# Splitting x two steps behind its load, and issuing ScalarE's transfers from GpSimd, in a fused linear-attention and feed-forward kernel

## Chip, cores, metric

One core of a Trainium2 chip. The metric is the device time of one execution in microseconds, as the median of several. The profile is a trace of one execution; its span is mostly some 1.8 us shorter than that execution's device time.

## The reference, cut to what matters

```python
def _attn_ref(q, k, v, alpha):            # (4, 8, 768, 48) each
    for t in range(S):
        state = alpha[:, :, t, :, None] * state + np.einsum('bhd,bhe->bhde', k[:, :, t], v[:, :, t])
        y[:, :, t] = np.einsum('bhd,bhde->bhe', q[:, :, t], state)

def _moe_ref(x, w1, w2, w3, w_out):       # x (3072, 384), w1 and w2 (384, 1024)
    a = x @ w1
    b = x @ w2
    h = a * b @ w3
    return h @ w_out
```

The attention's output, reshaped to 3072 tokens of 384, is the x of the second part. All is float32; the weights arrive as 64-bit floats.

## The kernel before

Part one walks over 24 chunks of 128 tokens. Step n makes the scores of chunk n, the attention of chunk n-1, the logarithms of n+4, the decays of n+3, and so on. Three chunks make a group of x (384 tokens, in DRAM tile `xd`). In part one a finished group is loaded back every four steps, beginning at step 4, split into three float32r parts, and fed to "gates" (tiles of `x @ w1` times `x @ w2`), which fill TensorE's spare time in later steps. A gate runs in two halves; `run(k)` advances k halves. `convert` advances the work that turns a weight tile from 64-bit words to float32 parts on DVE and ACT.

```python
    def decays(n):
        ...                                                          # a matmul on the logarithms la
        nc.scalar.activation(e[:, 0], lc, AF.Exp, scale=-1.0)        # L259
        nc.scalar.activation(e[:, 1], lc, AF.Exp)                    # L260
        if n in ends:
            nc.scalar.dma_start(out=ends[n][0:1], in_=e[0:1, 0])
    ...
    def split_x(g, i):
        x = st.pop(("xT", g))
        t = tr[i].tile([C, 3, KM, TG], FP32R, tag="x3", name="x3")   # one buffer in part one
        st["x3", g] = t
        nc.scalar.activation(t[:, 0], x, AF.Copy, scale=1.0 - 2.0 ** -13)             # L376
        nc.vector.tensor_sub(t[:, 1], x, t[:, 0].bitcast(FP32))                       # L377
        nc.vector.scalar_tensor_tensor(t[:, 2], t[:, 0].bitcast(FP32), 1.0 + 1.0 / P, x,
                                       op0=ALU.mult, op1=ALU.subtract)                # L378
    ...
    begin = {4 + 4 * g: (g, range(FH if g < 4 else KF)) for g in range(5)}
    for n in range(N + 1):
        ...
        if n < N:
            scores(n)                       # L330 on TensorE: its start marks step n below
        transposed(n + 1)                   # L290 on TensorE, L292 copies qkT on ACT
        if n - 1 in begin:
            g, tiles = begin[n - 1]
            split_x(g, 0)
            fill.extend(gate(g, f) for f in tiles)
        ...
        if n:
            attend(n - 1)                   # stores y to xd
        outer(n)
        run(n - 1 not in begin)
        decayed(n + 2)                      # L268 on DVE
        logs(n + 4)                         # L238 on ACT
        if n in begin:
            load_x(begin[n][0], nc.scalar)  # L370
        run(1)
        decays(n + 3)
        ...
        run(n - 1 in begin)
```

The framework that builds the kernel decides in which order the instructions of one engine stand in that engine's queue.

Of the kernel before, what the change touches and what calls it, by code (L numbers as in the profile page):

```python
# [48 lines left out]
def kernel(  # L49
# [12 lines left out]
    nc = tc.nc  # L62
    B, H, S, D = q.shape
    C = 128
# [5 lines left out]
    DP = 64  # L70
# [30 lines left out]
    def bank():  # L101
        return ps.tile([C, 512], FP32, tag="bank", name="bank")
# [6 lines left out]
    ends = {n: dram.tile([3, DM], FP32, name=f"ends{n}") for n in range(2, N, 2) if n % NCH}  # L109
# [11 lines left out]
    def load_a(n):  # L121
        if n < N:
            st["a", n] = inp.tile([C, H, D], FP32, tag="ac", name="ac")
            nc.sync.dma_start(out=st["a", n], in_=rows(alpha, n))

    def load_kq(n):
        if n >= N:
            return
        st["kq", n] = inp.tile([C, 2, H, D], FP32, tag="kq", name="kq")
        nc.sync.dma_start(out=st["kq", n][:, 0], in_=rows(k, n))  # L130
        nc.sync.dma_start(out=st["kq", n][:, 1], in_=rows(q, n))

    def load_v(n):
        if n < N:
            st["v", n] = vs[n % len(vs)]
            nc.sync.dma_start(out=st["v", n][:, :, 0:D], in_=rows(v, n))
# [22 lines left out]
    decs = [p1.tile([C, 3, NP], FP32, name=f"dec{i}") for i in range(2)]  # L159
# [54 lines left out]
    def convert(steps, ahead=3):  # L214

        for _ in range(steps):
            while weights and len(begun) < ahead:
                begun.append(weights.popleft())
                next(begun[-1])
            if not begun:  # L220
                return
            x = begun.popleft()
            try:
                next(x)
                begun.appendleft(x)
            except StopIteration:
                pass
# [5 lines left out]
    def logs(n):  # L233
        if n >= N:
            return
        a = st.pop(("a", n)).rearrange("p h d -> p (h d)")
        la = st["la", n] = work.tile([C, DM], FP32, tag="la", name="la")
        nc.scalar.activation(la, a, AF.Ln)  # L238
        if n >= LATE:

            t = st["la", n] = work.tile([C, 2, DM], FP32R, tag="la2", name="la2", bufs=1)
            nc.scalar.copy(t[:, 0], la)
            nc.vector.tensor_sub(t[:, 1], la, t[:, 0].bitcast(FP32))
        if n in ends:
            nc.scalar.dma_start(out=ends[n][2:3], in_=a[0:1])

    def decays(n):
        if n >= N:
            return
        lc = bank()[:, 0:DM]  # L250
        la = st.pop(("la", n))
        if n < LATE:
            nc.tensor.matmul(lc, utri if n % 2 else after, la, start=True, stop=True)
        else:
            for i in range(2):
                nc.tensor.matmul(lc, sums[:, n % 2], la[:, i], start=(i == 0), stop=(i == 1))  # L256

        e = st["e", n] = work.tile([C, 2, DM], FP32, tag="e", name="e", bufs=3)
        nc.scalar.activation(e[:, 0], lc, AF.Exp, scale=-1.0)  # L259
        nc.scalar.activation(e[:, 1], lc, AF.Exp)  # L260
        if n in ends:
            nc.scalar.dma_start(out=ends[n][0:1], in_=e[0:1, 0])
        if n + 1 in ends:
            nc.scalar.dma_start(out=ends[n + 1][1:2], in_=e[C - 1:C, 1])

    def decayed(n):
        if n < N:
# [3 lines left out]
    def load_ends(n):  # L271
        if n not in ends:
            return
        with nc.allow_non_contiguous_dma(reason="single values to partitions"):
            for i in range(2):
                nc.scalar.dma_start(out=decs[n // 2 % 2][ds(DP * i, D)].rearrange("d m j -> d (m j)"),
                                    in_=ends[n].rearrange("m (j i d) -> i d (m j)", i=2, d=D)[i])

    def transposed(n):
# [58 lines left out]
    def attend_state(n):  # L338
        qkT = st.pop(("qkT", n))



        y = [bank()[:, 0:HP * C].rearrange("p (j c) -> p j c", c=C) for _ in range(2)]
        st["y", n] = y, [(half * HP + j, i, y[i][ds(DP * half, DP), j, :])
                         for j in range(HP) for i in range(2) for half in range(2)]
        if n % NCH:
            for j, i, to in st["y", n][1]:
                r = ds(DP * i, D)
                nc.tensor.matmul(to, Ts[n % 2][r, j, :], qkT[r, 1, j, :],  # L349
                                 start=(j % HP == 0), stop=False, skip_group_check=True)  # L350

    def attend(n):
        (y, heads), ms, vc = st.pop(("y", n)), st.pop(("ms", n)), st.pop(("v", n))
        for j, i, to in heads:
            nc.tensor.matmul(to, vc[:, 2 * j + i, :], ms[:, i, j, :], start=(n % NCH == 0 and j % HP == 0),  # L355
                             stop=(j % HP == HP - 1), skip_group_check=True)
        x = work.tile([C, HP, 2, C], FP32, tag="x", name="x")
        for i in range(2):
            nc.scalar.copy(x[:, :, i], y[i])
        x = x.rearrange("p j i t -> p (j i) t")  # L360

        g, c = divmod(n, G)
        to = xd[g].rearrange("(b h d) t -> b d h t", b=2, d=D)
        for half in range(2):
            nc.scalar.dma_start(out=to[half, :, :, ds(c * C, C)], in_=x[ds(DP * half, D)])


    def load_x(g, queue=nc.sync):
        st["xT", g] = xp.tile([C, KM, TG], FP32, tag="xT", name="xT")
        queue.dma_start(out=st["xT", g], in_=xd[g].rearrange("(k p) t -> p k t", p=C))  # L370
# [10 lines left out]
    def exact(to, w, x, scale):  # L381

        p1, p2 = (bank()[:, 0:to.shape[1]] for _ in range(2))
        n = len(w[0])
        for part in range(2):
            for i in range(n):
                nc.tensor.matmul(p1, w[part][i], x[part][i], start=(part == i == 0), stop=(part == 1 and i == n - 1))  # L387
        t = gw.tile(list(to.shape), FP32, tag="t", name="t")
        nc.scalar.activation(t, p1, AF.Copy, scale=(1.0 + 1.0 / P) * scale)  # L389
        for i in range(n):  # L390
            nc.tensor.matmul(p2, w[2][i], x[2][i], start=(i == 0), stop=(i == n - 1))  # L391
        nc.vector.scalar_tensor_tensor(to, p2, -scale, t, op0=ALU.mult, op1=ALU.add)  # L392

    def gate(g, f):
        r = []
        x = [[st["x3", g][:, part, kk, :] for kk in range(KM)] for part in range(3)]
        for i, scale in enumerate((1.0, P * P)):
            r.append(gw.tile([C, TG], FP32, tag="r", name="r"))
            exact(r[-1], [[w12[:, part, i, kk, ds(f * C, C)] for kk in range(KM)] for part in range(3)], x, scale)
            if len(r) == 1:  # L400
                yield
        ab = abp.tile([C, TG], FP32, tag="ab", name="ab")
        nc.vector.tensor_mul(ab, *r)  # L403
        store_ab()
        st["ab"] = g, f, ab

    def store_ab():
        if "ab" in st:
            g, f, ab = st.pop("ab")
            nc.sync.dma_start(out=abd[g][:, f, :], in_=ab)  # L410
# [57 lines left out]
    def run(pieces):  # L468

        for _ in range(pieces):  # L470
            if not fill:
                return
            try:
                next(fill[0])
            except StopIteration:
                fill.popleft()
# [18 lines left out]
    load_kq(3)  # L495
    load_a(4)

    begin = {4 + 4 * g: (g, range(FH if g < 4 else KF)) for g in range(5)}

    for n in range(N + 1):  # L500
        load_v(n + AHEAD - 1)
        load_a(n + 5)
        load_kq(n + AHEAD)
        if n:
            attend_state(n - 1)
        if n < N:
            scores(n)
        transposed(n + 1)
        if n - 1 in begin:
            g, tiles = begin[n - 1]  # L510
            split_x(g, 0)
            fill.extend(gate(g, f) for f in tiles)
        if n == 0:
            logs(2)
            decays(2)
            logs(3)
        early = n < 7
        convert(1, 2 if n == 0 else 3)
        advance(n)
        if n:  # L520
            attend(n - 1)
        outer(n)
        run(n - 1 not in begin)
        if early:
            convert(1)
        decayed(n + 2)
        logs(n + 4)
        if n in begin:
            load_x(begin[n][0], nc.scalar)
        convert(early and n > 2)  # L530
        run(1)
        decays(n + 3)
        load_ends(n + 2)
        convert(early or n % 3 == 0)
        run(n - 1 in begin)
    part1.close()


# [78 lines left out]
```

## Time and profile before

| | before |
|---|---|
| device time, median of the first 3 runs | 507.94 us (507.48 to 508.53) |
| span of the profile | 506.9 us |
| PE busy | 466.6 us (92%), so 40.3 us idle |
| DVE, ACT, POOL busy | 371.3, 248.1, 13.8 us |
| mean granted TensorE clock | 0.973 |

The profile's lines are in the prediction. Read them for PE alone: from 215 us on PE is busy without gaps, but for one wait of 1.0 us at 403 us (L387 for `ab`, L454). So a change to part one can do little more than bring the start of that stretch forward.

### The profile page before, as it was taken

To read this page: it belongs to the slowest core of one execution; us is meant where nothing else is said; L and a number is where in the kernel's file an instruction comes from. 1 tells how busy PE (TensorE), PEld (TensorE's weight loads), DVE (VectorE), ACT (ScalarE), POOL (GpSimd) and SP (SyncE) were. 2 spreads that over 40 slices of the span, in tenths; PEclk is the share of its full clock that TensorE was granted. 3 is DMA by queue.
4 is the path that set the end of the run, shared out by engine and by line. 5 is a ranking of instruction groups with operands and counts; after the bars stand their busy time and mean duration, and the time that the engine had idled before them with its cause. 6 is when DMAs were issued, how large, how long until landed. Compare 5 with 4: busy or idle time off the path is not lost.

```text
span 506.9 us, 9883 instructions
## 1 busy us (share of the span) xinstructions
PE 466.6 (92%) x3760; PEld 424.8 (84%) x3760; DVE 371.3 (73%) x620; ACT 248.1 (49%) x479; POOL 13.8 (3%) x43
## 2 busy tenths in 40 slices
PE   3777499499799999999999999999999999999997
PEld 1556388398799899899999998898888799999996
DVE  2777789699966767599999976967533497777771
ACT  2665566468557555355555544544323343333330
POOL 2000000010100010000000000000000000000000
PEclk9998599889899999999999999999999999999999
DMA  9999999998879833265565432432001686555511
GB/s 173 182 217 196 256 216 225 194 246 209 166 167 215 194 81 106 79 186 174 177 200 186 160 117 88 142 103 72 33 31 48 171 231 192 174 180 179 174 56 47
DMA packets 168735, 79.10 MB, mean 156 GB/s; under 512 B 112856, under 2 KB 162544, under 8 KB 168688
## 3 DMA queue, kind: packets, MB, share of 16 engines
q1 hardware_dynamic: 147184, 70.73, 54.9%
q10 hardware_dynamic: 21504, 7.75, 6.7%
q8 instruction: 29, 0.48, 0.4%
q14 instruction: 18, 0.15, 0.1%
HBM read 56.40 MB, written 22.06 MB: 155 GB/s over the span
## 4 chain that ended last, share of the span: by engine, by line
PE 71%; DVE 1%; issue 0%; ACT 0%; DVEq 0%
PE bank L387 36%; PE bank L391 18%; PE bank L436 8%; PE bank L355 2%; PE bank L330 2%; PE bank L430 1%; PE bank L349 1%; PE bank L290 1%; PE bank L302 1%; PE bank L256 1%; DVE x L378 1%; DVE x L377 0%; ACT t L389 0%; ACT ab L454 0%; DVE r L392 0%
## 5 line engine op out<-in xcount | busy, mean ns | idle before, releaser
L387 PE MATMUL bank<-x,w 128*128 128x384 f32 x768 | 163.9, 348 | 15.0 <-DVE x L377 8.5
L387 PEld LDWEIGHTS bank<-x,w 128*128 128x128 f32 x768 | 136.5, 192 | 21.1 <-DVE x L377 9.7
L389 ACT ACTIVATE t<-bank 128x384 f32<-128x384 f32 x152 | 73.4, 490 | 119.2 <-PE bank L387 96.7
L392 DVE SCALAR_TENSOR_TENSOR r<-bank,t 128x384 f32<-128x384 f32 x128 | 68.4, 550 | 45.7 <-ACT t L389 37.1
L391 PE MATMUL bank<-x,w 128*128 128x384 f32 x384 | 89.2, 340 | 1.5 <-DVE x L378 1.4
L391 PEld LDWEIGHTS bank<-x,w 128*128 128x128 f32 x384 | 69.2, 191 | 3.1 <-PE bank L387 1.4
L387 PE MATMUL bank<-w3o,ab 128*128 128x384 f32 x384 | 70.6, 335 | 1.0 <-ACT ab L454 1.0
L387 PEld LDWEIGHTS bank<-w3o,ab 128*128 128x128 f32 x384 | 66.8, 188 | 1.4 <-ACT ab L454 1.3
L436 PE MATMUL bank<-wo,w3T 128*128 128x384 f32 x128 | 42.6, 486 | 0.0
L391 PE MATMUL bank<-w3o,ab 128*128 128x384 f32 x192 | 37.1, 334 | 0.0
L436 PEld LDWEIGHTS bank<-wo,w3T 128*128 128x128 f32 x128 | 24.2, 189 | 14.9
L189 ACT ACTIVATE rest<-raw 128x512 f32<-128x512 uint32 (+1 forms) x36 | 23.4, 649 | 26.6 <-DMA raw<-in_moe_w_dram 18.3
L455 DVE TENSOR_TENSOR ab<-abl,ab 128x1024 fp32r<-128x1024 f32 x24 | 29.4, 1223 | 9.1 <-ACT ab L454 9.1
L403 DVE TENSOR_TENSOR ab<-r 128x384 f32<-128x384 f32 x64 | 35.3, 552 | 0.9
L454 ACT ACTIVATE ab<-abl 128x1024 fp32r<-128x1024 f32 x24 | 25.5, 1062 | 20.1 <-PE bank L391 18.8
L330 PEld LDWEIGHTS bank<-qkT 48*128 48x128 f32 x384 | 25.5, 198 | 10.8 <-ACT qkT L292 5.1
L330 PE MATMUL bank<-qkT 48*128 48x128 f32 x384 | 30.7, 298 | 4.2 <-ACT qkT L292 3.7
L333 DVE TENSOR_TENSOR ms<-bank,keep 128x512 int32<-128x512 int32 x48 | 31.2, 682 | 4.2 <-PE bank L330 4.2
L391 PEld LDWEIGHTS bank<-w3o,ab 128*128 128x128 f32 x192 | 33.6, 188 | 0.0
L292 ACT COPY qkT<-bank 128x512 f32<-128x512 f32 x48 | 25.8, 586 | 10.3 <-PE bank L290 8.8
L194 ACT ACTIVATE power<-power,rebias 128x512 uint32<-128x512 uint32 (+1 forms) x36 | 25.0, 696 | 10.3 <-DVE power L193 10.3
L392 DVE SCALAR_TENSOR_TENSOR o<-bank,t 128x384 f32<-128x384 f32 x24 | 13.4, 556 | 22.1 <-issue 13.7
(65 smaller groups left out, 509.7 us busy)
## 6 DMA issues: line engine op xcount, KB each, us to landing
abd<-ab SPq DMA_DIRECT2D x64, 192.0 KB
abl<-abd SPq DMA_DIRECT2D x24, 512.0 KB
raw<-in_moe_w_dram SPq DMA_DIRECT2D x16, 512.0 KB
raw<-in_moe_w_dram SPq DMA_DIRECT2D x24, 256.0 KB
ac<-in_alpha_dram SPq DMA_DIRECT2D x24, 192.0 KB
kq<-in_k_dram SPq DMA_DIRECT2D x24, 192.0 KB
kq<-in_q_dram SPq DMA_DIRECT2D x24, 192.0 KB
v<-in_v_dram SPq DMA_DIRECT2D x24, 192.0 KB
```

Of the source, the lines that this page charges most:

```text
L194: nc.scalar.activation(power, power, AF.Relu, scale=2.0 ** 23, bias=rebias)
L292: nc.scalar.copy(qkT[:, :, :, ds(DP * half, DP)], tp[half])
L330: nc.tensor.matmul(sc[i][:, j, :], qkT[r, 0, j, :], qkT[r, 1, j, :], start=True, stop=True)
L333: nc.vector.tensor_tensor(ms[:, i].bitcast(I32), sc[i].bitcast(I32), keep_bc, op=ALU.bitwise_and)
L387: nc.tensor.matmul(p1, w[part][i], x[part][i], start=(part == i == 0), stop=(part == 1 and i == n - 1))
L389: nc.scalar.activation(t, p1, AF.Copy, scale=(1.0 + 1.0 / P) * scale)
L391: nc.tensor.matmul(p2, w[2][i], x[2][i], start=(i == 0), stop=(i == n - 1))
L392: nc.vector.scalar_tensor_tensor(to, p2, -scale, t, op0=ALU.mult, op1=ALU.add)
L403: nc.vector.tensor_mul(ab, *r)
L436: nc.tensor.matmul(po, w3T[:, j, :], wo[:, j, :], start=(j == 0), stop=(j == KF - 1))
L454: nc.scalar.activation(t[:, 0], ab, AF.Copy, scale=1.0 - 2.0 ** -13)
L455: nc.vector.tensor_sub(t[:, 1], ab, t[:, 0].bitcast(FP32))
```

## The change

Its intent: give the split of x a whole step of slack after the load, so that PE never stands before a gate whose x isn't split, keep gates out of the step that splits, and take the issuing of transfers out of ScalarE's queue. All 93 transfers of ScalarE move.

```diff
-            nc.scalar.dma_start(out=ends[n][2:3], in_=a[0:1])
+            nc.gpsimd.dma_start(out=ends[n][2:3], in_=a[0:1])
 ... the same at the stores of e, the loads of dec, the stores to xd and load_x
-        if n - 1 in begin:
-            g, tiles = begin[n - 1]
+        if n - 2 in begin:
+            g, tiles = begin[n - 2]
             split_x(g, 0)
             fill.extend(gate(g, f) for f in tiles)
+        pieces = (0, 3, 3, 2)[(n - 6) % 4] if n > 5 else 0
 ...
-        run(n - 1 not in begin)
+        run(pieces > 0)
 ...
-        run(1)
+        run(pieces > 1)
 ...
-        run(n - 1 in begin)
+        run(pieces > 2)
```

## The prediction

> **What bounds the kernel now.** I read the page first (part 4, then part 2), then PE's waits, PE's instructions in order of time, and last the busy table of chosen stretches. The chain that ended last is nearly all TensorE, so an idle or slow microsecond of PE is a microsecond of the kernel:
>
> ```profile
> PE 71%; DVE 1%; issue 0%; ACT 0%; DVEq 0%
> PE   3777499499799999999999999999999999999997
> DMA  9999999998879833265565432432001686555511
> ```
>
> From slice 17 on (215 us) PE is full; four dips lie before that, under a DMA row that is full up to slice 10. The waits of PE from 40 to 215 us name the dips:
>
> ```profile
> PE bank L387 <- DVE x L377: 8.5, 3, 4.8
> PE bank L387 <- ACT x L376: 6.5, 2, 4.8
> PE bank L391 <- DVE x L378: 1.4, 2, 0.8
> ```
>
> That is 16.4 us of PE waiting for the split of x (one ACT copy, two DVE operations), out of some 20 us idle in that stretch. In order of time, PE's rows at the second split (the first row is the last attention work of the step):
>
> ```profile
> 92.29 0.62 PE L302 MATMUL bank<-v,qk 128*64 128x48 f32 x16
> 94.65 0.79 PE L387 MATMUL bank<-x,w 128*128 128x384 f32 x3 [1.74 <-ACT x L376]
> 100.28 1.33 PE L387 MATMUL bank<-x,w 128*128 128x384 f32 x3 [4.84 <-DVE x L377]
> ```
>
> The gates stand in PE's queue in the same step as the split, and PE takes its queue in order, so the next chunk's attention waits too. Taking the start of each score group (L330) as the start of step n, the split steps 5, 9, 13, 17, 21 last 18.6, 17.4, 12.0, 8.0 and 7.0 us, against 7.3 of an ordinary step with one gate. **The excess is 11.3 + 10.1 + 4.7 + 0.7 + 0 = 27 us**: the waits, and matmuls at a low clock after them.
>
> Why was the split late? DVE's rows there:
>
> ```profile
> 95.53 0.43 DVE L190 TENSOR_SCALAR mant<-raw 128x512 uint32<-128x512 uint32 x1 [4.75 <-DMA raw<-in_moe_w_dram]
> 98.88 1.35 DVE L377 TENSOR_TENSOR x<-xT,x 128x1152 fp32r<-128x1152 f32 x1
> ```
>
> x had been requested at 76.0 us; DVE stood in line behind a weight tile that DMA had not delivered. So the splits are late because DMA and DVE are behind, which matters for what can be won. The busy table, before and after the last large dip:
>
> ```profile
> core 0: us, PE busy (x) PEld busy (x) DVE busy (x) ACT busy (x) POOL busy (x), PEclk, DMA share, GB/s
> 47.60:140.40 92.80, 75.27 (x840) 66.11 (x838) 80.00 (x140) 57.88 (x125) 5.44 (x9) 0.86 0.99 214
> 140.40:215.00 74.60, 73.77 (x962) 67.75 (x959) 49.51 (x87) 40.39 (x93) 3.43 (x9) 1.00 0.59 141
> ```
>
> In the first stretch PE has 75 us of work, partly at a clock of 0.86, DVE 80, and DMA is full: three engines near their limit. In the second PE alone binds, and only 0.8 us of it is lost.
>
> **What the Trainium skill says.** (1) "DMA: Bandwidth & Descriptors", section "Issuing engines are not separate DMA queues": transfers from any engine share the same 16 DMA engines, and another issuer saves only sequencer time. So no bandwidth comes from the move. The trace of before agrees in that ACT and SP together reach 214 GB/s. (2) Same page, "SWDGE vs HWDGE vs iDMA": a transfer issued by GpSimd has its descriptors written in software; "Latency and other measured facts" gives about 1 us to the first byte instead of 0.6. The kernel before has no GpSimd transfer, so nothing here shows it. (3) "SBUF — State Buffer", the box on DVE blocking DMA: GpSimd can't write descriptors while DVE runs a two-port operation. The candidates are the integer operations of the weight conversion, 0.42 us each, so a delay of well under 1 us each time. No trace shows it yet. (4) "TensorE: Matmul & The Clock Gate", section on the HAM clock gate: after some 3.4 us idle the array falls to half clock. The trace agrees: the three matmuls after the 4.8 us wait take 1.33 us, where a warm triple takes about 0.7.
>
> **The change, part by part.**
>
> *Transfers.* 93 leave ACT: 48 stores of x, 5 loads of x, 40 small ones. Their rows in ACT's order of time sum to 38 us up to 215 us (mean 0.41, longest 2.2). ACT is 58 busy in 93 us, so most of this lay beside other work. It cost PE only through single late evictions: waits of 0.8 + 0.6 + 0.4 = 1.8 us behind L392 and L389. I count 1 us of gain. On GpSimd, 93 issues at an estimated 1 to 1.5 us (from the skill's first-byte figure) are 90 to 140 us of a 215 us stretch in which it did 14 us of work. It fits. The state update on GpSimd (L321, eight times) now queues behind transfers, but has about one step between the product it needs and the next sum.
>
> *Split a step later, gates 0, 3, 3, 2 halves.* One gate is 3.3 us of PE (L387 at 150.79 to L256 at 154.06). A step without gates is 4.1 us of PE. Four steps carry the same 29.5 us as before. But at any step after the first split, the changed kernel is one gate (3.3 us) behind in work, which is done after 215 us: positions must be compared minus 3.3.
>
> - Steps 5 and 6 have no gates. DVE binds them: mask 1.3, qk 0.95, state 0.35, one weight tile 4.2 make 6.8 us; step 6 adds a split (2.7) and a difference (0.55) to give 10.1. Step 7 starts near 47.6 + 17 = 64.6, where it was 73.2; two gates undone (6.6). Gain 2.0.
> - Steps 7 to 9: 3 x 4.1 + 4 x 3.3 = 25.5, so step 10 starts at 90, where it was 106.3. Minus 3.3: gain so far 13.
> - Steps 10 to 13: DVE had 22.1 + 11.2 = 33.3 us in these steps before, and they lasted 34.1. Against PE's 29.5, DVE binds: step 14 at about 123.5 where it was 140.4, gain so far 13.6. DMA: it moved 19.8 MB from 47.6 to 140.4 us; I take 1.5 MB as fetched ahead of need. 18.3 MB at the 225 GB/s of its fullest stretches are 81 us, so step 14 can't start before about 129, that is 11.4 before its old place, or 8 after the gate owed. I take the middle of 8 and 13.6, 10.8.
> - Steps 14 and 18: these step groups were at PE's pace. A step with 4.1 us of PE now holds DVE for 1.3 + 2.7 + 0.35 + 0.95 + 0.55 = 5.85, behind an ACT copy of 1.2; the transposes of the next step need the qk that DVE makes after the split. I estimate 2 us of PE idle at 14, 18 and 22 each, less the 0.8 that is saved: loss 5. The scheduler may fill part of it with gates: I count 3.
>
> Sum: 1 + 10.8 - 3 = 8.8 us. After 215 us nothing changes: PE has the same work plus the gate already counted. **507.9 - 8.8 is 499 us**, ratio 0.982.
>
> **Rivals.** (a) *The whole 27 us comes back* (about 481 us). For it: the waits name only the split. Against: DMA share 0.99 and DVE at 80 of 93 us in the same stretch; when the split no longer stops PE, the next chunk's loads do. (b) *Nothing comes back* (505 to 508): DMA sets the pace to 140 us, and the stalls were only where PE noticed it. For it: DMA at 1.0 or more up to 106 us, DVE and ACT waiting for raw weights and alpha. Against: during the 17.4 us of step 9 the loads ran on and filled buffers, and PE was gapless in steps 6 to 8 and 10 to 12. (c) *GpSimd becomes a wait* (508 to 520): the 16 loads of single values have 576 four-byte pieces each; if software needs several us for one, the state update behind it comes late and holds DVE and then PE.[...] Against: eight updates only, each with about 7 us of room. (d) *The light steps starve PE and the heavy ones don't make it up*: 2 us at each of five, taking the gain down to 3 to 5 us.
>
> **Range and chances.** The middle is 499. Rival (d) with (b) gives the upper side, 507; half of rival (a)'s remainder gives 491. The line of 2% is 497.8, 1.2 below my number, so faster is a little under even: 0.42; same 0.53; slower 0.05, which only (c) could bring.
>
> **What would show it.** Right: PE's waits for L376 to L378 fall from 16.4 us to under 3; the dips at 50 to 60 and 90 to 100 us are filled, PE's clock between 47 and 140 us is above 0.9; part one of the kernel (the last score group) ends near 200 us instead of 206 and PE is gapless after it; ACT shows no transfers, a third queue appears; new PE waits of 1 to 2 us at L290 or L330 for ACT qkT or DVE qk, in the steps without gates. Wrong: PE's gaps in 50 to 140 us as long as before but named otherwise (alpha, qkT), which is (b); GpSimd busy above half, with DVE waiting for POOL T, which is (c); a DMA share under 0.9 between 47 and 106 us would mean that software descriptors slow the loads. A time under 490 would show that DMA's fullness was no limit at all.

## The result

| | before | after |
|---|---|---|
| device time, median of 4 runs | 508.21 us | 509.46 us |
| span of the profile | 506.9 us | 507.9 us |
| PE busy | 466.6 us | 472.9 us |
| PE idle (span less busy) | 40.3 us | 35.0 us |
| POOL busy | 13.8 us | 70.6 us |
| mean granted TensorE clock | 0.973 | 0.966 |

The ratio is 1.0032, with a 95% interval of 1.001 to 1.0054. The time stayed within 2%, if anything a little longer, and lay outside the predicted range of 491 to 507 us.

The page of the changed kernel, its 40 slices (tenths of busy time, of the granted clock, of the DMA engines):

```profile
PE   3888479999899999999999999999999999999997
PEclk9989579979979999999999999999999999999999
DMA  9999998899895642466555533321100676665511
...
q0 software_dynamic: 4304, 7.75, 5.8%
```

The dip at slice 8 of the old PE row (89 to 101 us) is filled; the one at slice 5 (51 to 63 us) is as deep as before, and slice 6 behind it fell from 9 to 7. The transfers moved to a software queue, with all their 7.75 MB. PE's waits from 40 to 215 us in the changed kernel (total, times, longest):

```profile
PE bank L253 <- ACT la L238: 7.5, 1, 7.5
PE bank L290 <- DVE qk L268: 4.8, 3, 3.3
PE bank L256 <- DVE la L243: 2.2, 2, 1.3
PE bank L330 <- ACT qkT L292: 0.8, 1, 0.8
```

The waits for the split, 16.4 us before, are all gone. **New waits stand in their place, 15.3 us in these four rows**, and none of them is for a gate. The largest, in order of time, is here: first PE's rows, then ACT's (start, duration, what; in brackets the idle time before and what ended it).

```profile
48.58 1.09 PE L355 MATMUL bank<-ms,v 128*64 128x128 f32 x16
57.17 1.65 PE L253 MATMUL bank<-la,after 128*128 128x384 f32 x2 [7.50 <-ACT la L238]
```

```profile
48.14 0.49 ACT L260 ACTIVATE e<-bank 128x384 f32<-128x384 f32 x1
55.54 1.16 ACT L376 ACTIVATE x<-xT 128x1152 fp32r<-128x1152 f32 x1 [6.91 <-DMA xT<-xd]
56.61 0.51 ACT L238 ACTIVATE la<-ac 128x384 f32<-128x384 f32 x1
```

This is the key reading. In the kernel before, the same rows of ACT's queue were:

```profile
49.74 0.53 ACT L238 ACTIVATE la<-ac 128x384 f32<-128x384 f32 x1 [1.19 <-DMA ac<-in_alpha_dram]
...
55.50 0.59 ACT L292 COPY qkT<-bank 128x512 f32<-128x512 f32 x1
55.98 1.17 ACT L376 ACTIVATE x<-xT 128x1152 fp32r<-128x1152 f32 x1
```

**The first split (L376) is not two steps behind its load in ACT's queue.** It stands in step 5, directly behind the exponentials and ahead of the logarithm L238. ACT takes its queue in order, so it stood 6.9 us in front of an x that was still on its way, and PE stood 7.5 us behind ACT for a logarithm whose input was there. GpSimd's rows show why x came when it did:

```profile
49.17 0.95 POOL L370 DMA_DIRECT2D xT<-xd  x1 [3.07 <-DMA xd<-x]
```

The load could go out only when the stores to `xd` had landed, at 49.17 us, and landed some 6 us later. In the kernel before the same split started at almost the same time, 55.98 us, but behind L238 and both qkT copies, so that only gates waited for it.

The Trainium skill has the rule, "TensorE: Matmul & The Clock Gate", section "Architectural detail: the array is 16× 32×32, not 1× 128×128": ACT's and DVE's queues are strict first-in-first-out. The trace agrees (the 6.91 us). The prediction reasoned so about PE's queue and not about ACT's.

The second kind of wait, on DVE in step 7:

```profile
65.66 1.35 DVE L377 TENSOR_TENSOR x<-xT,x 128x1152 fp32r<-128x1152 f32 x1
66.93 1.35 DVE L378 SCALAR_TENSOR_TENSOR x<-x,xT 128x1152 fp32r<-128x1152 f32 x1
68.20 0.35 DVE L310 COPY T<-bank 128x192 f32<-128x192 f32 x1
68.47 0.68 DVE L209 SCALAR_TENSOR_TENSOR w<-w,mant 128x512 fp32r<-128x512 f32 x1
69.07 0.68 DVE L210 SCALAR_TENSOR_TENSOR w<-w,mant 128x512 fp32r<-128x512 f32 x1
69.67 0.95 DVE L268 TENSOR_TENSOR qk<-kq,e 128x768 f32<-128x768 f32 x1
```

DVE has no gap here; the product L268 that the next transposes need comes behind two operations of the split and two of a weight tile, and PE waits 3.33 us for it, until 70.76 us. Step 7 has three half gates, but they stand behind these transposes in PE's queue (the first starts at 73.32 us), so PE has nothing else to do.

Where the starts of the score groups stand (us, from the trace, of several kernels that follow below):

| kernel | step 10 | step 14 | step 18 | step 22 | span |
|---|---|---|---|---|---|
| before | 106.3 | 140.4 | 170.4 | 198.8 | 506.9 |
| after | 96.5 | 133.7 | 168.5 | 198.0 | 507.9 |
| e1_schedule_only | 97.1 | 129.7 | 163.4 | 195.0 | 505.0 |
| e3_split_behind_step | 93.1 | 129.6 | 164.2 | 194.1 | 504.0 |
| e9_hold_scalar | 91.7 | 127.1 | 163.7 | 193.7 | 503.6 |
| e4_even_gates | 90.0 | 128.6 | 161.2 | 190.1 | 499.8 |
| e7_even_on_scalar | 96.5 | 129.4 | 161.7 | 194.8 | 504.6 |
| e10_light_dve (wrong) | 93.1 | 127.0 | 162.4 | 191.9 | 501.9 |
| e12_even_light_weights (wrong) | 87.3 | 121.4 | 154.8 | 183.7 | 493.4 |

All kernels but the first owe one gate (3.3 us, see the prediction) at these places. So the changed kernel is really 9.8 - 3.3 = 6.5 us ahead at step 10, 3.4 at 14, 1.4 **behind** at 18 and 2.5 behind at 22. It won time early and gave it back.

### The profile page after: what moved, and what is told of

Same layout as the page of the kernel before. It is cut to its first block, busy times and chain, and to the rows that moved or that the text cites. A ratio compares the mean times of both kernels' runs of the same rounds, so it can differ in the third digit from the quotient of the medians.

```text
span 507.9 us, 9943 instructions
## 1 busy us (share of the span) xinstructions
PE 472.9 (93%) x3760; PEld 431.7 (85%) x3760; DVE 371.8 (73%) x620; ACT 248.8 (49%) x479; POOL 70.6 (14%) x136
## 3 DMA queue, kind: packets, MB, share of 16 engines
q0 software_dynamic: 4304, 7.75, 5.8%
## 4 chain that ended last, share of the span: by engine, by line
PE 73%; DMA 9%; DVE 9%; ACT 3%; issue 3%; SPq 2%; POOL 1%; ACTq 0%; POOLq 0%; DVEq 0%
PE bank L387 37%; PE bank L391 18%; PE bank L436 8%; DMA raw<-in_moe_w_dram 3%; PE bank L330 2%; PE bank L355 2%; DMA dec<-ends 2%; DMA ends<-e 2%; PE bank L430 1%; DMA xT<-xd 1%; DVE ms L333 1%; PE bank L290 1%; PE bank L349 1%; DVE r L392 1%; DMA raw<-in_moe_w_out_dram 1%
## 5 line engine op out<-in xcount | busy, mean ns | idle before, releaser
L387 PE MATMUL bank<-x,w 128*128 128x384 f32 x768 | 160.5, 343 | 0.0
L391 PE MATMUL bank<-x,w 128*128 128x384 f32 x384 | 87.6, 335 | 1.0 <-DVE ms L333 0.6
L330 PEld LDWEIGHTS bank<-qkT 48*128 48x128 f32 x384 | 28.7, 221 | 11.2 <-ACT qkT L292 5.0
L330 PE MATMUL bank<-qkT 48*128 48x128 f32 x384 | 34.1, 323 | 3.9 <-ACT qkT L292 3.2
L436 PEld LDWEIGHTS bank<-wo,w3T 128*128 128x128 f32 x128 | 24.2, 189 | 14.9
L365 POOL DMA_DIRECT2D xd<-x x48 | 28.8, 603 | 48.1 <-ACT x L359 46.2
L454 ACT ACTIVATE ab<-abl 128x1024 fp32r<-128x1024 f32 x24 | 25.5, 1062 | 19.0 <-PE bank L391 18.8
```

What stands on the lines that cost most here:

```text
L330: nc.tensor.matmul(sc[i][:, j, :], qkT[r, 0, j, :], qkT[r, 1, j, :], start=True, stop=True)
L365: nc.gpsimd.dma_start(out=to[half, :, :, ds(c * C, C)], in_=x[ds(DP * half, D)])
L387: nc.tensor.matmul(p1, w[part][i], x[part][i], start=(part == i == 0), stop=(part == 1 and i == n - 1))
L391: nc.tensor.matmul(p2, w[2][i], x[2][i], start=(i == 0), stop=(i == n - 1))
L436: nc.tensor.matmul(po, w3T[:, j, :], wo[:, j, :], start=(j == 0), stop=(j == KF - 1))
L454: nc.scalar.activation(t[:, 0], ab, AF.Copy, scale=1.0 - 2.0 ** -13)
```

## The experiments

Two theories at the start. **Order** (S): in the queues of ACT and DVE the split stands ahead of work that the attention chain needs. **Supply** (D): DMA and DVE are the pace up to step 14, and any gain ahead of that is lost again; a rival to both is **GpSimd** (G), whose software-made transfers might come late. Thirteen kernels ran; each ratio is against the kernel before on the same chip.

### One half of the change at a time

e1_schedule_only: the new schedule, transfers left on ScalarE.

```diff
-nc.gpsimd.dma_start(...)     # at every transfer that the change had moved
+nc.scalar.dma_start(...)
```

> The changed kernel with all 93 transfers given back to ScalarE, so only the new schedule of split and gates. Theory S (the schedule itself eats its gain: the first split still stands right behind its load in ACT's queue, and the steps without gates leave PE idle and at a low clock): 503 to 510 us, PE again at a clock under 0.9 in the steps without gates. Theory G (transfers whose descriptors GpSimd writes come late and hold the rest): 500 us or less, and PE's waits small. Theory D (DMA sets the pace up to 140 us): 506 to 510 us.

e2_gpsimd_only: the kernel before with all 93 transfers on GpSimd.

```diff
-nc.scalar.dma_start(...)     # at every transfer of ScalarE
+nc.gpsimd.dma_start(...)
```

> The kernel before with only the 93 transfers moved from ScalarE to GpSimd. S: 506 to 512 us, since PE's waits for the split stay, and the first split has moved forward in ACT's queue to the same place as in the changed kernel, so its wait gets longer by some us. G: 511 us or more. D: 507 to 509 us.

Measured: e1 504.99 us, ratio 0.9923 (0.9898 to 0.9948). e2 507.21 us, ratio 0.9962 (0.9947 to 0.9977). **Each half alone is faster; both together are slower.** The halves add to -1.15% and the whole is +0.32%, some 7 us apart. GpSimd as issuer is refuted as a culprit in the old schedule; in the new one the kernel with it is 1.1% slower than the one without (1.0032 against 0.9923). Both times lie in the ranges of S, e2's in that of D as well. In e1 the first split ran at the end of step 6, right behind the qkT copies, and found its x landed:

```profile
62.47 1.07 ACT L292 COPY qkT<-bank 128x512 f32<-128x512 f32 x2
63.42 1.18 ACT L376 ACTIVATE x<-xT 128x1152 fp32r<-128x1152 f32 x1
```

Yet the program lines around the split are the same in e1 and in the changed kernel. What differs is who issues the transfers, and with that the order in which ACT's queue was built. e2 has the split early in ACT's queue too, but there the gates behind it were what waited, as before (6.8 us for L376).

### The split held back in the queues

e3_split_behind_step: the changed kernel with the split as the last thing of its step, and its instructions held behind that step's exponential on ACT and product on DVE. e6_split_line_only moves the line alone, without the hold. e9_hold_scalar moves the line and holds ACT's copy only.

```diff
-        if n - 2 in begin:                     # ahead of attend
-            g, tiles = begin[n - 2]
-            split_x(g, 0)
-            fill.extend(gate(g, f) for f in tiles)
 ...                                            # last lines of the step:
+        if n - 2 in begin:
+            g, tiles = begin[n - 2]
+            with tc.issue_after(st["exp"].ins), tc.issue_after(st["mul"].ins):   # not in e6
+                split_x(g, 0)
+            fill.extend(gate(g, f) for f in tiles)
```

> The changed kernel, its split held back in the queues of ACT and DVE behind the exponentials and the qk product of its step (issue order only), gates and transfers as they were. S: the 7.5 us wait of PE for alpha in step 5 goes, and PE's waits for la, ms and qk in the steps without gates shrink: 499 to 503 us. G and D: nothing that they name is changed, 507 to 511 us.

> The changed kernel with the split moved to the last line of its step in the program, but not held back in the queues: the first split stays at the same row of ACT's queue as in the changed kernel. Theory O (what counts is the row in the queue, which the scheduler chooses): little is won, 506 to 510 us, with a wait of ACT for the load of x of over 3 us in step 5. Rival (the place in the program is what counts): 503 to 506 us, as with the split held back.

> The changed kernel with the split called in the last line of its step and only ScalarE's copy of it held behind that step's exponentials; the two DVE operations are not held. DVE's order as built equals the one of the run that moved the line alone (507.9 us) in the first two splits; only ScalarE's order differs from that run: the first split stands 14 rows later. If the copy's place in ScalarE's queue is what cost, 505 to 506 us, as with both parts held (505.4). If the DVE part is what mattered, 507.5 to 508.5, as with the line moved alone.

Measured: e3 505.42 us, 0.9933 (0.9908 to 0.9958); e6 507.86 us, 0.9976 (0.9934 to 1.0019); e9 506.21 us, 0.9939 (0.9924 to 0.9953). The changed kernel had 1.0032. e3 fell between the ranges of the theories (499 to 503 and 507 to 511 us): the order gave back only part of what S had expected. e6 is in the range of its theory O, e9 just above that for the copy. In e6 the split's copy still stood ahead of L238 in ACT's queue, and PE's wait shows it; in e3 it runs without waiting, behind the exponential of its own step. First e6's largest wait of PE, then e3's (40 to 215 us):

```profile
PE bank L253 <- ACT la L238: 6.8, 1, 6.8
```

```profile
PE bank L349 <- DVE ms L333: 3.0, 2, 1.6
PE bank L391 <- DVE x L378: 2.8, 3, 1.6
```

```profile
60.25 0.51 ACT L260 ACTIVATE e<-bank 128x384 f32<-128x384 f32 x1
60.62 1.19 ACT L376 ACTIVATE x<-xT 128x1152 fp32r<-128x1152 f32 x1
```

So the order in the queues cost about 1% (1.0032 to 0.9933), and holding the ACT copy is enough to get it back. How much of that is the copy and how much are DVE's two operations isn't clean: the interval of e6 touches both. A correction to what I had written ahead of e9: DVE's order in it agrees with that of e6 to within one row at the first split, but at the second DVE's part stands some 12 rows later, as in e3. The hold on ACT moves DVE's part too, because that needs ACT's result. e9 shows that the hold on DVE adds nothing measurable; it doesn't isolate ACT.

### Even gates

e4_even_gates: e3, but the split comes at the end of the step after the load (a step sooner), and every step runs two halves. e7_even_on_scalar is e4 with the transfers back on ScalarE.

```diff
-        pieces = (0, 3, 3, 2)[(n - 6) % 4] if n > 5 else 0
+        pieces = 2
 ...
-        if n - 2 in begin:                     # at the end of the step, held
-            g, tiles = begin[n - 2]
+        if n - 1 in begin:
+            g, tiles = begin[n - 1]
```

> As the run with the split held back, but with two half gates in every step instead of 0, 3, 3, 2; the split comes at the end of the step after its load, behind that step's last gate. S: no step is short of PE work, PE stays at full clock from the first gates on: 494 to 499 us. G: 505 us or more. D: 505 us or more.

> Even gates with the split held back, with all 93 transfers on ScalarE. If GpSimd's transfers cost time (G): 497 us or less. If moving them is worth the 2 us that it was worth in the kernel before: 501 to 504 us. If the order of the queues was all that mattered: 499 to 502 us, the same as even gates on GpSimd.

Measured: **e4 500.69 us, 0.9835 (0.9801 to 0.9868)**, the fastest correct kernel, ahead of both. It takes another 1% off e3: from step 14 to step 22 it loses 3.1 us against the kernel before (a lead of 11.8 us becomes 8.7), where e3 loses 6.1 and the changed kernel 5.9. That fits the prediction's light steps that starve PE, with 3 us of the loss from the uneven split of gates, but it isn't shown: e7, as even, loses 6.9 us there, and e1, uneven, 6.8, both with ScalarE's transfers. The whole step from e3 to e4 also holds the earlier split, which was not tried alone. The expected 494 to 499 us were missed by 1.7 us.

e7: 506.46 us, 0.9941 (0.9906 to 0.9976), slower than all three of its expectations. With the split held and the gates even in both, GpSimd as issuer is worth 1%, not the 1 us of the prediction. The same holding and evening that took the changed kernel from 1.0032 to 0.9835 brought nothing on ScalarE (e1 0.9923, e7 0.9941), so the parts of the change don't add. ACT's rows in e7 show how a transfer in its queue holds its work (rows of ACTq are issues):

```profile
49.64 0.52 ACT L238 ACTIVATE la<-ac 128x384 f32<-128x384 f32 x1 [0.92 <-DMA ac<-in_alpha_dram]
52.65 0.24 ACTq L245 DMA_DIRECT2D ends<-ac  x1
52.94 0.66 ACT L189 ACTIVATE rest<-raw 128x512 f32<-128x512 uint32 x1 [2.77 <-DMA xT<-xd]
...
56.72 0.24 ACTq L264 DMA_DIRECT2D ends<-e  x1
57.00 0.59 ACT L292 COPY qkT<-bank 128x512 f32<-128x512 f32 x1 [1.56 <-DMA raw<-in_moe_w_dram]
```

ACT did nothing from 50.2 to 52.9 us, and an issue stands right at the end of that gap, as again before the second qkT copy; PE then waited 4.89 us for qkT. The issue itself takes 0.24 us, so what costs is the gap ahead of it, in which what stands behind it can't run. For what the issue at 52.65 us waited isn't settled: the profile names the load of x, which the issue doesn't need.

### The clock

e5_keep_warm: the changed kernel with eight useless matmuls (128x384, 336 ns each) in each of the steps 6, 10 and 14.

```diff
         outer(n)
+        if n in (6, 10, 14):
+            waste = bank()[:, 0:TG]
+            for _ in range(8):
+                nc.tensor.matmul(waste, sums[:, 1], junk.rearrange("p i c -> p (i c)"), start=True, stop=True)
```

> The changed kernel with eight useless matmuls (128x384, some 1.3 us at full clock) put into PE's queue in steps 6, 10 and 14, just ahead of the place where PE idles for la. Theory C (the steps without gates cost mainly because PE's clock halves after them): the matmuls of steps 11 and 15 run at full clock, PE's busy time without the useless ones falls from 472.9 to 467 to 470 us, and the time stays at 506 to 510 us although 3.9 us of work are added. Rival I (only idle time matters, the clock little): PE busy without them stays at 472 or more, the time is 509 to 513.

The reason to try it: the change cut PE's idle time by 5.3 us, yet PE's busy time rose by 6.3 us for the same 3760 matmuls, at a lower clock. Measured: 512.37 us, 1.0083 (1.003 to 1.0136). The time is in the range of rival I. But PE's busy time is 471.6 us, 5.0 of them for the useless matmuls, and the other 466.6 us are even under what theory C had expected: each of the two was right in one sign. The busy table of e5 below gives, in order, the stretch, PE busy, PEld, DVE, ACT, POOL, the clock, the DMA share and GB/s; first the changed kernel, then e5:

```profile
140.40:215.00 74.60, 73.41 (x880) 68.07 (x881) 48.72 (x84) 39.43 (x89) 24.14 (x43) 0.95 0.55 127
```

```profile
140.40:215.00 74.60, 72.63 (x913) 65.93 (x910) 52.77 (x90) 40.19 (x92) 26.84 (x45) 1.00 0.59 137
```

The clock is restored from 0.95 to 1.00 there, and the kernel takes 2.9 us more. 6.3 us of PE's other work were saved, 5.0 were added, and PE's idle time rose from 35.0 to 38.4 us. So what the clock gave went into waits: the lower clock looks like a mark of the starved steps more than their price. The run doesn't isolate this, since the useless matmuls hold PE's queue themselves.

### What limits the steps up to 14

Four kernels that are wrong, and below them one try to improve e4. e8_light_weights: the changed kernel with nine of the twelve weight tiles of the gates loaded to one eighth of their columns. e10_light_dve: the changed kernel without two DVE operations on each of these tiles. e12_even_light_weights and e13_even_light_dve: the same two edits on e4.

```diff
-            nc.sync.dma_start(out=raw[:, ds(i * m, m)], in_=src)          # e8, e12
+            k = m if full else m // 8        # raw: three fixed buffers, filled once by full loads
+            nc.sync.dma_start(out=raw[:, ds(i * m, k)], in_=src[:, 0:k])
```

```diff
-        nc.vector.scalar_tensor_tensor(mant, top, 2.0 ** -20, rest, ...)        # L196; e10, e13
-        nc.vector.scalar_tensor_tensor(power, high, 0x80000000, power, ...)     # L197
+        if dst is not None:                  # no longer for the tiles of the gates
+            ... the same two
```

> The changed kernel, wrong on purpose: nine of the twelve weight tiles of the gates load only an eighth of their columns (the rest of the buffer keeps old words), which takes some 4.1 MB of transfers out of the first 105 us, with every compute instruction kept. D (the loads set the pace up to about 100 us): 499 us or less. S (split order and steps without gates): 504 to 509 us.

> Wrong on purpose: the changed kernel without the two operations L196 and L197 on every weight tile of the gates (2 x 0.68 us of the 4.2 us that DVE works on such a tile, 12 tiles, some 16 us of DVE in all). If DVE's work is what the light steps run into now, 500 to 504 us, and the starts of the score groups 10 to 14 come 3 us or more sooner; if the order in the queues (the split's copy waiting for x ahead of the logarithm) or DMA is what counts, 507 to 510.

> Wrong on purpose: the version with even gates and the split held back (500.7 us, step 14 at 128.6 us) with nine of twelve gate weight tiles loaded to an eighth (some 4 MB less before step 14). With the splits no longer in the way, if DMA's bytes set the start of step 14 (the prediction's floor of 129 us), step 14 starts at 122 to 126 and the time is 494 to 498 us. If DVE or something else sets it, step 14 stays at 127 to 130 and the time at 499 to 501.

> Wrong on purpose: the same version without L196 and L197 on the gate weight tiles (some 16 us of DVE less before step 14). If DMA sets the start of step 14, it stays at 127 to 130 us and the time at 499 to 501. If DVE sets it, step 14 starts at 122 to 126 and the time is 494 to 498 us. If each of the two runs brings a part, both limits lie close together.

Measured: e8 503.32 us, 0.9894 (0.9864 to 0.9925); e10 503.99 us, 0.9901 (0.9856 to 0.9946); e12 494.49 us, 0.9696 (0.967 to 0.9722); e13 498.82 us, 0.981 (0.9761 to 0.986).

On the changed kernel both edits bring about 1.3%. e10 is what DVE as the limit had let expect, in time and in places (step 10 3.4 us and step 14 6.7 us sooner), so there DVE's work counts as much as the bytes; yet PE still waited 6.1 us for the logarithm (L238 in the other kernels), and in e8 the split still stood 4.8 us in ACT's queue. Once the order is mended they part. Less DVE work moves e4 by 1.9 us (within the intervals, the record's verdict is "unclear", and its profiled run was its slowest, so I read no positions from it); fewer bytes move it by 6.2 us, and step 14 comes 7.2 us sooner. e8 fell between what the two theories had expected of it, with DVE full in its place (84.9 of 92.8 us from 47.6 to 140.4 us). The busy table from step 5 to 10 and 10 to 14, first of e4, then of e12 (columns as above):

```profile
49.12:89.98 40.86, 36.01 (x455) 31.35 (x451) 38.02 (x68) 27.24 (x59) 19.14 (x30) 0.96 1.03 228
89.98:128.58 38.60, 31.98 (x372) 27.70 (x368) 31.52 (x55) 23.91 (x53) 9.82 (x19) 0.96 0.99 232
```

```profile
48.90:87.27 38.37, 34.81 (x455) 29.95 (x451) 38.37 (x70) 29.68 (x64) 18.36 (x30) 1.00 1.04 208
87.27:121.41 34.14, 30.99 (x372) 27.26 (x368) 32.81 (x59) 23.42 (x52) 11.93 (x20) 0.95 0.89 203
```

In e4 the DMA engines are full in both stretches, while DVE has 9.9 us of idle time: 40.86 x 228 + 38.60 x 232 is 18.3 MB, so step 14 comes when the bytes have come, at 128.6 us. The prediction had 18.3 MB at 225 GB/s and 129 us. In e1, e3, e4 and e7, four kernels with different orders and gates, step 14 starts between 128.6 and 129.7 us. It isn't a sharp floor: e9 gets there at 127.1 and e10 at 127.0 us, and at a DMA share of 1.00 to 1.03 the rate from step 10 to 14 was 226 GB/s in e1, 237 in e9 and 239 in e7. In e12 only 14.9 MB come in these stretches, and now DVE is full: 38.37 of 38.37 us, then 32.81 of 34.14, with a DMA share that is still 1.04 and then 0.89. The two limits lie close together, in e4 DMA first. That is close to what the supply theory had expected of both runs (e12's step 14 came 0.6 us sooner than its range, e13's time 0.2 us below its own).

e11_even_pool: e4 with the last multiplication of the gates' weight tiles on GpSimd.

```diff
-        nc.vector.tensor_mul(to, mant, power.bitcast(FP32))
+        (nc.gpsimd if dst is None else nc.vector).tensor_mul(to, mant, power.bitcast(FP32))
```

> The version with even gates and the split held back (500.7 us), with the last multiplication of each gate weight tile (0.68 us on DVE) moved to GpSimd. If DVE is its limit up to step 14, 498 to 500 us. If GpSimd is much slower at it (over 2 us a tile) or its transfers come late behind it, 501 to 505.

Measured: 506.56 us, 0.9943 (0.9928 to 0.9958), worse than e4 by 1.1%, and slower than both expectations. The operation takes 1.28 us on GpSimd where DVE took 0.69, and PE's 4.2 us wait for L238 came back with it. So 5.9 us were lost, where 12 x 0.69 = 8.3 us of DVE work had been taken away. The trace shows how at this wait, first on GpSimd, then on ACT:

```profile
51.30 0.77 POOL L370 DMA_DIRECT2D xT<-xd  x1 [4.78 <-DMA xd<-x]
52.09 1.27 POOL L199 TENSOR_TENSOR mant<-mant,power 128x512 f32<-128x512 f32 x1
```

```profile
53.39 0.63 ACT L207 ACTIVATE w<-mant 128x512 fp32r<-128x512 f32 x1 [4.00 <-POOL mant L199]
```

The multiplication stood in GpSimd's queue behind the load of x, which waited for the stores; ACT's L207 waited for the product, and the logarithm L238 stood behind L207. It is the same fault as in the changed kernel, on another engine. How much of the 5.9 us it made was not taken apart.

## Why the prediction was wrong

- **The bound of the kernel before**: right. The waits for the split went to zero, and PE stayed gapless after 215 us.
- **Freeing ACT, 1 us**: the term doesn't stand alone. In the old schedule it is 0.4% (e2), with the split held and even gates 1.1% (e4 against e7), in the new schedule -1.1% (the changed kernel against e1). I had counted only evictions that PE waited for, and not the idle stretches of ACT that end with an issue (2.8 us in one place in e7, 2.71 in the kernel before), nor PE's waits for L260 and L238 (1.9 and 0.8 us). The "longest 2.2" is a row of two issues; the longest single store issue took 1.14 us.
- **GpSimd's cost**: the rival was rightly given little. The 93 issues took 0.52 to 0.81 us in the mean, by kind, instead of the 1 to 1.5 that I had estimated, and POOL was busy 70.6 us in all.
- **Steps 5 and 6 bound by DVE, step 7 at 64.6 us**: measured 66.3, near by luck. Step 5 took 13.1 us and not 6.8, through ACT's wait for x; step 6 took 6.5 and not 10.1.
- **Steps 7 to 9 at PE's pace, step 10 at 90 us**: this failed; it was 96.5, with 3.3 us of PE waiting for the product behind the split on DVE. With the split held and the gates even, step 10 starts at 89.98 (e4), but there the split also comes a step sooner.
- **Step 14 at 123.5 or 129 us, the middle taken as 10.8 us of gain**: the DMA sum was nearer than the middle. It gives 8 us, and e1, e3, e4 and e7 have 7.3 to 8.5 (e9 has 10.0); that the bytes set this place in e4 is shown by e12. The changed kernel has 3.4: the queue order costs it the other 4 (7.5 with the split held, e3).
- **Light steps lose 3 us**: they lost 5.9. With even gates 3.1 are lost on GpSimd (e4), 6.9 on ScalarE (e7).
- **The sum.** Predicted 10.8 - 3 + 1 = 8.8 us of gain. Measured in the spans: 3.4 at step 14, less 5.9 up to step 22, plus 1.5 from there to the end: -1.0. The last 1.5 come with ScalarE's transfers too (1.4 in e1), so they aren't the ACT term. 1.0 of them is PE's wait for L454 at 403 us, which only the kernel before and e2 have; I have no cause for the rest.

**The step that failed** is the first of "Split a step later": steps 5 and 6 bound by DVE, with the split in step 6. I took the line in the program for the place in the queue. A split called a step later stood in step 5, earlier in ACT's queue than before; ACT waited 6.9 us there, PE 7.5 us, step 5 took 13.1 us instead of 6.8, and what waited was the attention chain and no longer the gates. The loss of the light steps and the middle between two limits, above, were mis-sized as well: even with the order mended (e3) the ratio is 0.9933 and not 0.982. The outcome looks like rival (b) by its sign, gaps as long as before but named otherwise; e3 and e9 show that they were the order's and not only DMA's. My list of rivals held a version of this (qk and qkT behind the split in light steps), but with 2 us each and only from step 14. The range's lower chance of slowness (0.05) rested on GpSimd as a wait, which in the changed kernel's trace holds PE for 0.19 us (T of L321, at 46.15 us); what GpSimd did bring was another order in ACT's queue.

What stays open: the halves' 7 us of disagreement. The order explains about 1%, 5 us, of it; the rest isn't assigned. Nor is it known why even gates and the held split win 2% with GpSimd's transfers and nothing with ScalarE's.

## What to carry to other kernels

Before you count what a moved line is worth, look at where its instruction stands in the queue of each in-order engine: an operation that waits for a transfer must stand behind everything on that engine that feeds the critical chain. A wait that disappears from a list of waits is worth nothing until you have seen what stands in its place. And when a supply limit (bytes by GB/s) and an engine limit give two places for the same event, take the later one, not the middle: here it came within 2 us in e1, e3, e4, e7 and e9, the kernels whose ACT queue had lost its fault (not in e11).

## What the Trainium skill lacked or had wrong

- "DMA: Bandwidth & Descriptors", "Issuing engines are not separate DMA queues", says that another issuer saves only sequencer time. The rate fits that (from 47.6 to 140.4 us 226 GB/s in e4 with GpSimd, 223 in e7 with ScalarE), but the page doesn't warn that the issuer changes what stands behind what in a compute queue: an issue in ScalarE's queue stood at the end of a 2.8 us gap of its compute (e7), and GpSimd as issuer was worth 1.1% in e4 against e7 and cost 1.1% in the changed kernel against e1.
- No page has the cost of an issue on GpSimd's own queue by kind of transfer. Here it was 0.60 us for a 96 KB store, 0.52 us for one of a single row, 0.71 us for a load of single values, and 0.81 us for the load of x (means).
- The same page, "Anatomy of one DMA — SWDGE (gpsimd) path", fits 2.0 us plus the bytes over 436 GB/s: 2.2 us for 96 KB. Under the DMA load of this kernel the median from issue to landing was 4.2 us.
- "SBUF — State Buffer", the box on DVE blocking DMA: no run here shows harm from it. From 47.6 to 140.4 us, with DVE busy 75 to 84 of 93 us, all eight correct kernels with GpSimd's transfers kept a DMA share of 0.90 to 1.02. Whether DVE ran in a two-port mode isn't seen in the traces, so this doesn't refute the box.
- "TensorE: Matmul & The Clock Gate", the HAM clock gate: the prediction took from it that the clock halves after some 3.4 us of idle time. Here less was enough: in the changed kernel it was 0.50 from 104 to 109 us, after waits of PE of 1.29 and 0.25 us with one matmul between them. The page also lacks a warning that a restored clock may win nothing: brought from 0.95 to 1.00 by 5.0 us of useless matmuls, the kernel was 2.9 us slower.
